# Strided heads of two batches regrouped by residue into small TensorE tiles, and local heads five chunks at a time

## The chip, the cores and the metric

One core of one Trainium2 chip runs the whole program in a single launch. The metric is the device time of that launch in microseconds. Three runs of the kernel before took 805.01, 805.74 and 808.72 us, a median of 805.74 us.

## What is computed

Attention with two kinds of heads, and then a token-and-channel mixer (an MLP over tokens, one over channels). Batch 8, 8 heads, 576 positions, 64 values per head:

```
scores = q @ k.T / 8
local heads 0-3:   key j counts for query i when 0 <= i-j < 32
strided heads 4-7: key j counts when j <= i and j % 32 == i % 32
attn = softmax(scores); x = attn @ v, heads side by side: x is [8, 576, 512]
h = relu(x.T @ w_tok1) @ w_tok2          (576 -> 256 -> 576 over tokens)
u = x + h.T
out = u + relu(u @ w_ch1) @ w_ch2        (512 -> 1536 -> 512 over channels)
```

## The kernel before, in words

The mixer works on fp32r pairs (a high and a low part, three matmuls for a product). It runs batch by batch: `mlp` (L705) takes 12 blocks of the hidden width, an up projection (`up_proj`, L720, 12 matmuls of 512 columns into the one PSUM bank `h`) and a down projection (`down_proj`, L742, 12 matmuls) each. A table `after` of this batch puts small pieces of other work between these steps: entry 3 is called when three projections have been written, and 3.5 in the middle of the fourth. The order on TensorE, VectorE, ScalarE and GpSimd is the order in which the code is written; before the first `mlp` that of the DMA queue on SyncE is too.

A strided head splits by residue: 32 residues, and 18 positions in each, so its scores are 32 causal blocks of 18x18. For batches 2 to 7 GpSimd and VectorE do them (`strided`, L388). For batches 0 and 1 TensorE does: `strided_pe` (L332) takes seven residues at once, so that 126x126 scores come out of one matmul, and the mask (an identity times `mask2_b`, L342, bf16) shuts what lies off the 18x18 diagonal blocks. One call handles one head (`j` of a pair `hp`) and the groups `gs`, three of them or two (`GS`, L616). It yields twice: after the scores and the exponential (L342 to L350), and after the transposes (L354) and their copy (L356); then come the products with the values (L360) and the division (L365 to L367). The result goes to the DRAM tensor `xd` (L372), and batch 0 loads it back into the SBUF tile `x` (`load_x`, L473).

Batch 0's local heads are done by `local_unit` (L180), for three or two chunks of 128 positions, in 64x32 tiles of the array: scores L197, transposes L224, values L232. Half a chunk belongs to batch 1; its first half is copied into `x` by DMA (L255). All this stands before the first `mlp`, together with the loading of the weights. A weight arrives as 64-bit floats and `convert` (L106) makes fp32r pairs of it, piece by piece: two operations on ScalarE (L128, L131), two on VectorE (L129, L133), then a cast on ScalarE (L142) and a subtraction on GpSimd (L143). The pieces are two and a short one of `t1` (w_tok1), two and a tail of `t2` (w_tok2), and of `w1` and `w2` (the channel weights); the first four of `w1` are also made here.

`tok1` (L481) splits the five chunks of `x` into high and low (L490, L496) and multiplies by `t1`; `hh` (L516) and `hl` (L517) are its result. `tok2` (L536) transposes one 128-column slice of `x` into PSUM, adds six matmuls with `t2` (L547), and `split_u` casts the sum to `uh` (L525, ScalarE) and `ul` (L526, VectorE), which the first `up_proj` reads.

Batch 1's strided heads are two `lanes` (L784), called in batch 0's `mlp` after steps 0 to 11 and half a step later, and what is left of batch 0's local heads (`rest`, L795) is called there as well. They share the three PSUM banks `t`.

Of the kernel before, what the change touches and what calls it, by code (L numbers as in the profile page):

```python
# [16 lines left out]
ALU = mybir.AluOpType  # L17
# [17 lines left out]
BUSY = 8  # L35
RG = 7
RP = RG * NJ
NRG = 5
NSB = 2
FIRST = {0: 1, 4: 2}  # L40
# [18 lines left out]
def attn_mixer_kernel(ctx, tc, qkT, vw, qkU, vU, qs, ks, vs, qksT, vsP, mask, mask2, w1, w2, wt1, wt2, outT):  # L59
# [14 lines left out]
    mask2_b = small[:RP, 64 + 16:64 + 16 + 3 * RP // 2].bitcast(BF16)  # L74
# [105 lines left out]
    def local_unit(pool, ps_t, p, hp, c0, n, into=None, single=(), masks=None, room=UC):  # L180

        one = dict.fromkeys(single, 1)
        qk_t = pool.tile([P, 2, room * P + 32], F32, name="lqk", bufs=one.get("lqk"))[:, :, :n * P + 32]
        q_t, k_t = qk_t[:, 0, 32:], qk_t[:, 1]
        v_t = pool.tile([P, 4 * room, DV], F32, name="lv")[:, :4 * n]
# [4 lines left out]
        if masks is not None:  # L190
            for j in range(2):
                nc.tensor.matmul(
                    sc[j][:, :64 * n], ident_b, masks[:, 64 * c0:64 * (c0 + n)], start=True, stop=False, skip_group_check=True)
        for t in range(4 * n):
            c, a = divmod(t, 4)
            for j in range(2):
                nc.tensor.matmul(  # L197
                    sc[j][32 * a:32 * a + 32, 64 * c:64 * c + 64],
                    q_t[64 * j:64 * j + 64, 32 * t:32 * t + 32], k_t[64 * j:64 * j + 64, 32 * t:32 * t + 64],
                    start=masks is None, stop=True, skip_group_check=True)  # L200
        s_t = pool.tile([P, room, 2, 64], F32, name="ls")
        m_t = pool.tile([P, room, 2], F32, name="lm")[:, :n]
        z_t = pool.tile([P, room, 2], F32, name="lz")[:, :n]
        if masks is not None:
            for j in range(2):
                s = sc[j][:, :64 * n].rearrange("p (c k) -> p c k", k=64)
                nc.vector.tensor_reduce(out=m_t[:, :, j], in_=s, axis=AX.X, op=ALU.max)
                nc.vector.tensor_tensor(
                    out=s_t[:, :n, j], in0=s, in1=m_t[:, :, j:j + 1].to_broadcast([P, n, 64]), op=ALU.subtract)
            s = s_t[:, :n].rearrange("p c j k -> p (c j k)")  # L210
            nc.scalar.activation(out=s, in_=s, func=AF.Exp, scale=SCALE)
        else:

            for c in range(n):
                for j in range(2):
                    nc.vector.tensor_tensor_reduce(
                        out=s_t[:, c, j, :], in0=sc[j][:, 64 * c:64 * c + 64], in1=mask_sb[:, FIRST.get(c0 + c, 0), :],
                        scale=-SCALE, scalar=TOP, op0=ALU.add, op1=ALU.min, accum_out=m_t[:, c, j:j + 1])
                    nc.scalar.activation(
                        out=s_t[:, c, j, :], in_=s_t[:, c, j, :], func=AF.Exp, bias=m_t[:, c, j:j + 1], scale=-1.0)  # L220
# [5 lines left out]
        nc.scalar.copy(out=pT[:, :n * P], in_=pt[:, :n * P])  # L226
# [12 lines left out]
        x_t = pool.tile([P, max(n - 1, 2) if into is not None or n < UC else UC, 2, D], F32, name="lx", bufs=one.get("lx"))  # L239
        cs = slice(P * hp, P * hp + P)  # L240

        nd = 0 if into is None else min(n, S // P - c0)
        for i0, i1 in ((0, nd), (nd, n)):
            for j in range(2):
                if i0 < i1:
                    to = x_t[:, i0:i1, j, :] if i0 >= nd else into[:, c0 + i0:c0 + i1, P * hp + D * j:P * hp + D * j + D]
                    nc.vector.tensor_tensor(
                        out=to, in0=av[j][:, i0:i1, :D],
                        in1=z_t[:, i0:i1, j:j + 1].to_broadcast([P, i1 - i0, D]), op=ALU.mult)
        if nd == n:  # L250
            return
        if nd:
            x = x_t[:, nd].rearrange("p j d -> p (j d)")
            for r in range(2):
                nc.sync.dma_start(out=into[64 * r:64 * r + 64, NSC - 1, cs], in_=x[:64])  # L255
            nc.sync.dma_start(out=xd[0][S:S + 64, cs], in_=x[64:])
            return
        nc.sync.dma_start(
            out=xd[p][P * c0:P * (c0 + n), cs].rearrange("(c p) d -> p c d", p=P), in_=x_t[:, :n].rearrange("p c j d -> p c (j d)"))
# [64 lines left out]
    def strided_load(pool, b, hp):  # L324
        one = 1 if b else 2
        qk_t = pool.tile([P, 2, S], F32, name="eqk", bufs=one)
        v_t = pool.tile([RP, NRG, 2, DV], F32, name="ev", bufs=one)
        nc.sync.dma_start(out=qk_t, in_=qksT[b, hp])
        nc.sync.dma_start(out=v_t, in_=vsP[b, hp])
        return qk_t[:, 0], qk_t[:, 1], v_t  # L330

    def strided_pe(pool, ps_t, b, hp, j, gs, loaded, outs):  # L332
        js = slice(64 * j, 64 * j + 64)
        q_t, k_t, v_t = loaded
        n = len(gs)

        rows = [min(RP, S - RP * g) for g in gs]
        sc = ps_t.tile([P, 512], F32, name="t")
        s_t = pool.tile([RP, 3, RP], F32, name="es", bufs=2 if b else 5)[:, :n]
        mz = pool.tile([RP, 2, 3], F32, name="em", bufs=2 if b else 5)[:, :, :n]  # L340
        m_t, z_t = mz[:, 0], mz[:, 1]
        nc.tensor.matmul(sc[:RP, :RP * n], ident_b[:RP, :RP], mask2_b[:, :RP * n], start=True, stop=False, skip_group_check=True)  # L342
        for i, g in enumerate(gs):
            r = rows[i]
            nc.tensor.matmul(  # L345
                sc[:r, RP * i:RP * i + r], q_t[js, RP * g:RP * g + r], k_t[js, RP * g:RP * g + r], start=False, stop=True, skip_group_check=True)
        s = sc[:RP, :RP * n].rearrange("p (c k) -> p c k", k=RP)
        nc.vector.tensor_reduce(out=m_t, in_=s, axis=AX.X, op=ALU.max)
        nc.vector.tensor_tensor(out=s_t, in0=s, in1=m_t.unsqueeze(2).to_broadcast([RP, n, RP]), op=ALU.subtract)
        nc.scalar.activation(out=s_t, in_=s_t, func=AF.Exp, scale=SCALE)  # L350
        yield
        pt = ps_t.tile([P, 512], F32, name="t")
        for i in range(n):
            nc.tensor.transpose(pt[:RP, RP * i:RP * i + RP], s_t[:, i], ident[:RP, :RP])  # L354
        pT = s_t
        nc.scalar.copy(out=pT, in_=pt[:RP, :RP * n].rearrange("p (c k) -> p c k", k=RP))  # L356
        yield
        av = ps_t.tile([P, 512], F32, name="t")
        for i, g in enumerate(gs):
            nc.tensor.matmul(av[:RP, DV * i:DV * i + DV], pT[:, i], v_t[:, g, j], start=True, stop=True)  # L360
        if j == 0:
            outs[gs] = pool.tile([RP, n, 2, D], F32, name=f"ex{n}", bufs=1 if b else 2)
        x_t = outs[gs]
        a = av[:RP, :DV * n].rearrange("p (c d) -> p c d", d=DV)
        nc.vector.tensor_scalar_add(z_t, a[:, :, D], 1e-9)  # L365
        nc.vector.reciprocal(out=z_t, in_=z_t)
        nc.vector.tensor_tensor(out=x_t[:, :, j], in0=a[:, :, :D], in1=z_t.unsqueeze(2).to_broadcast([RP, n, D]), op=ALU.mult)  # L367
        if j == 1:

            to = x_strided(b, P * hp, P).rearrange("(j r) d -> r j d", r=ST)  # L370
            for i, g in enumerate(gs):
                nc.sync.dma_start(out=to[RG * g:RG * g + rows[i] // NJ], in_=x_t[:rows[i], i].rearrange("p j d -> p (j d)"))  # L372
        yield


# [240 lines left out]
    GS = ((0, 1, 2), (3, 4))  # L616
    with tc.tile_pool(name="first", bufs=4) as first, \
         tc.tile_pool(name="raws", bufs=4, side="right") as raws, \
         tc.tile_pool(name="ps_a", bufs=6, space=PSUM) as ps_a, \
# [3 lines left out]
        mask2_sb = first.tile([RP, RP], F32, name="mask2_sb", bufs=1)  # L623
        masks = first.tile([P, 5 * 64], BF16, name="masks", bufs=1)
        nc.sync.dma_start(out=mask2_sb, in_=mask2)
        loaded = [strided_load(first, 0, hp) for hp in range(2)]
        nc.sync.dma_start(out=mask_sb, in_=mask)
        nc.gpsimd.tensor_copy(
            out=mask2_b.rearrange("p (c k) -> p c k", k=RP), in_=mask2_sb.unsqueeze(1).to_broadcast([RP, 3, RP]))
        for c in range(5):  # L630
            nc.gpsimd.tensor_copy(out=masks[:, 64 * c:64 * c + 64], in_=mask_sb[:, FIRST.get(c, 0)])
# [7 lines left out]

        keep_busy(WARM)  # L640
# [5 lines left out]
        for hp in range(2):  # L646
            outs = {}
            work += [strided_pe(first, ps_a, 0, hp, j, gs, loaded[hp], outs) for j in range(2) for gs in GS]
# [17 lines left out]
        for i in range(len(work) + 4):  # L666
            for k in (0, 2, 4):
                if 0 <= i - k < len(work):
                    if k == 2 and i >= BUSY:
                        keep_busy(2)  # L670
# [329 lines left out]
```

## Time and profile before

| | |
|---|---|
| median of three runs | 805.74 us |
| the profiled execution | 805.1 us, its span 803.3 us |
| TensorE busy | 781.1 us (97%) |
| VectorE, ScalarE, GpSimd busy | 476.6, 247.9, 378.0 us |
| first matmul of the first up projection | 52.92 us |
| granted TensorE clock | 1.00 in every stretch |
| DMA | 96.17 MB, mean 120 GB/s |

Busy time counts a matmul from its issue to its modelled end, and matmuls overlap, so "busy" alone does not say that the array is full. The chain that ended last gives TensorE 76% of the span, VectorE 10%, GpSimd 5%, DMA 4%.

### The profile page before, as it was taken

The page shows a single profiled execution, that of the slowest core. Times are in us where ns is not written, and L with a number is a line of the kernel's source. Part 1 is how long each engine was busy: PE and PEld are TensorE (multiplying, and loading weights), DVE is VectorE, ACT ScalarE, POOL GpSimd, SP SyncE. Part 2 cuts the span into 40 slices and gives each one's busy share as a digit, 9 for nine tenths or more (in the row PEclk, how much of TensorE's full clock was granted, in tenths as well). Part 3 has the DMA queues.
Part 4 walks back from the last instruction along what each step waited for, and adds up shares of the span by engine and source line. Part 5 has one row for each costly group of instructions (what it writes and reads, how often), then busy time and mean ns, then how long its engine had stood idle before and what let it go on. Part 6 is the DMA issues. An engine that isn't in the chain of part 4 may idle for free.

```text
span 803.3 us, 14310 instructions
## 1 busy us (share of the span) xinstructions
PE 781.1 (97%) x5714; PEld 632.0 (79%) x5718; DVE 476.6 (59%) x1030; ACT 247.9 (31%) x515; POOL 378.0 (47%) x285
## 2 busy tenths in 40 slices
PE   9789999999999999999999999999999999999998
PEld 6567776877778888888788888788888888888886
DVE  6856766778598677776687657776652233113112
ACT  5668765232122322331223122332222212102010
POOL 2223345959776883778558856766600000202000
PEclk9999999999999999999999999999999999999999
DMA  9676545234812282247215520655042212101001
GB/s 312 194 255 208 188 147 193 92 130 138 261 40 95 85 238 67 109 113 262 94 53 173 148 82 12 215 163 158 1 125 75 83 47 73 53 0 53 1 0 53
DMA packets 70782, 96.17 MB, mean 120 GB/s; under 512 B 33604, under 2 KB 42948, under 8 KB 70716
## 3 DMA queue, kind: packets, MB, share of 16 engines
q1 hardware_dynamic: 70140, 93.36, 37.3%
q10 hardware_dynamic: 576, 1.90, 0.6%
q8 instruction: 45, 0.74, 0.4%
q14 instruction: 21, 0.17, 0.1%
HBM read 67.65 MB, written 27.46 MB: 118 GB/s over the span
## 4 chain that ended last, share of the span: by engine, by line
PE 76%; DVE 10%; POOL 5%; DMA 4%; issue 2%; ACT 2%; SPq 1%; DVEq 0%; ACTq 0%; POOLq 0%
PE acc L740 30%; PE h L728 27%; PE t L547 5%; POOL sprod L383 4%; PE t L508 4%; PE t L728 3%; DMA w_raw<-in_w 2%; PE t L345 1%; DVE sa L463 1%; PE t L303 1%; DMA x<-x 1%; DVE xhl L496 1%; DVE w_f L133 1%; PE t L279 1%; DVE gl L732 1%
## 5 line engine op out<-in xcount | busy, mean ns | idle before, releaser
L383 POOL TENSOR_TENSOR sprod<-sa,ss 128x576 f32<-128x576 f32 (+8 forms) x108 | 153.3, 1457 | 84.8 <-issue 48.8
L383 POOL TENSOR_TENSOR sprod<-sa 128x576 f32<-128x576 f32 (+8 forms) x108 | 160.5, 1519 | 37.4 <-DVE ss L436 11.6
L740 PE MATMUL acc<-gh,w2h 128*128 128x512 f32 x432 | 170.7, 395 | 0.0
L732 DVE SCALAR_TENSOR_TENSOR gl<-h,gh 128x512 fp32r<-128x512 f32 x99 | 68.0, 687 | 172.9 <-ACT gh L731 172.8
L740 PE MATMUL acc<-gl,w2h 128*128 128x512 f32 x432 | 168.4, 390 | 0.0
L740 PE MATMUL acc<-gh,w2l 128*128 128x512 f32 x432 | 168.4, 390 | 0.0
L728 PE MATMUL h<-uh,w1h 128*128 128x512 f32 x396 | 157.9, 399 | 2.5 <-DVE gl L732 2.5
L728 PE MATMUL h<-ul,w1h 128*128 128x512 f32 x396 | 154.5, 390 | 0.0
L728 PE MATMUL h<-uh,w1l 128*128 128x512 f32 x396 | 154.5, 390 | 0.0
L731 ACT ACTIVATE gh<-h 128x512 fp32r<-128x512 f32 x99 | 59.0, 596 | 290.0 <-PE h L728 289.8
L436 DVE TENSOR_REDUCE ss<-sprod 128x9 f32<-128x576 f32 (+8 forms) x108 | 80.4, 777 | 28.0 <-POOL sprod L383 27.9
L740 PEld LDWEIGHTS acc<-gh,w2l 128*128 128x128 f32 x432 | 81.1, 188 | 17.2
L740 PEld LDWEIGHTS acc<-gh,w2h 128*128 128x128 f32 x432 | 81.1, 188 | 17.1
L740 PEld LDWEIGHTS acc<-gl,w2h 128*128 128x128 f32 x432 | 81.1, 188 | 16.4 <-DVE gl L732 0.3
L728 PEld LDWEIGHTS h<-uh,w1h 128*128 128x128 f32 x396 | 74.3, 188 | 20.5 <-DVE gl L732 4.1
L463 DVE TENSOR_REDUCE sa<-sprod 128x64 f32<-128x576 f32 (+8 forms) x108 | 80.1, 776 | 17.2 <-POOL sprod L383 16.8
L728 PEld LDWEIGHTS h<-ul,w1h 128*128 128x128 f32 x396 | 74.3, 188 | 16.0
L728 PEld LDWEIGHTS h<-uh,w1l 128*128 128x128 f32 x396 | 74.4, 188 | 14.5
L575 POOL TENSOR_TENSOR x<-x,xhl 128x512 f32<-128x512 f32 x4 | 5.0, 1288 | 115.2 <-DMA x<-u 115.2
L508 PE MATMUL t<-xhl,t1h 128*128 128x512 f32 x134 | 42.3, 398 | 4.7 <-DVE xhl L493 2.5
L496 DVE TENSOR_TENSOR xhl<-x,xhl 128x512 fp32r<-128x512 f32 x30 | 31.1, 1055 | 10.7 <-ACT xhl L490 10.7
L490 ACT CAST xhl<-x 128x512 fp32r<-128x512 f32 x37 | 22.3, 620 | 43.3 <-PE t L508 36.9
(141 smaller groups left out, 915.2 us busy)
## 6 DMA issues: line engine op xcount, KB each, us to landing
out_t<-ot SPq DMA_DIRECT2D x35, 256.0 KB
w_raw<-in_w SPq DMA_DIRECT2D x17, 512.0 KB
lqk<-in_qkU SPq DMA_DIRECT2D x9, 832.0 KB
x<-x SPq DMA_DIRECT2D x28, 256.0 KB
lv<-in_vU SPq DMA_DIRECT2D x9, 780.0 KB
xhl<-in_w SPq DMA_DIRECT2D x7, 512.0 KB
x<-lv SPq DMA_DIRECT2D x36, 96.0 KB
xtl<-lv SPq DMA_DIRECT2D x36, 96.0 KB
```

Source lines behind the costliest of these rows:

```text
L133: nc.vector.scalar_tensor_tensor(out=a, in0=a, scalar=3, in1=y, op0=ALU.logical_shift_left, op1=ALU.bitwise_xor)
L383: i = nc.gpsimd.tensor_tensor(op=op, **operands)
L436: nc.vector.tensor_reduce(out=s_t[:, i, :i + 1], in_=pr.rearrange("p (n d) -> p n d", d=D), axis=AX.X, op=ALU.add)
L463: nc.vector.tensor_reduce(out=o_t[:, i], in_=pr.rearrange("p (d n) -> p d n", n=i + 1), axis=AX.X, op=ALU.add)
L490: nc.scalar.copy(out=xh, in_=x)
L496: apart.append(nc.vector.tensor_tensor(out=xlo, in0=x, in1=xh.bitcast(F32), op=ALU.subtract))
L508: nc.tensor.matmul(ph[m], l[:, c, P * m:P * m + P], r, start=(c == 0 and k == 0), stop=(c == NSC - 1 and k == 1))
L547: nc.tensor.matmul(pu, l[:, cs], r[:, m, :MAIN], start=(turned and m == 0 and k == 0), stop=(m == 1 and k == 2), skip_group_check=True)
L728: nc.tensor.matmul(ph, l[:, cc, fs], r, start=(cc == 0 and k == 0), stop=(cc == NCC - 1 and k == 2))
L731: nc.scalar.activation(out=gh, in_=ph, func=AF.Relu)
L732: nc.vector.scalar_tensor_tensor(out=gl, in0=ph, scalar=0.0, in1=gh.bitcast(F32), op0=ALU.max, op1=ALU.subtract)
L740: nc.tensor.matmul(acc[cc], l[:, fc, cs], r, start=(fc == 0 and k == 0), stop=(fc == NFC - 1 and k == 2))
```

## The change

The strided heads of batches 0 and 1 are laid out in another way. The 32 residues are split into four groups of eight (`NB`); group `a` writes to PSUM partitions 32a to 32a+31, of which 18 are used. One matmul makes the scores of one residue of one head: 64 rows, 32 weight columns (18 used), 18 moving columns, in a 64x32 tile, 64 matmuls for a pair of heads. Four 128x128 transposes follow for the pair, and 64 matmuls with the values with 18 rows each, in two halves (`l0`). The values come with 18 partitions per load in four loads per pair, and the result leaves in four stores per pair. Both heads of a pair go through one reduction, one subtraction and one exponential.

```diff
-    def strided_pe(pool, ps_t, b, hp, j, gs, loaded, outs):
...
+    def strided_pe(pool, pair, one, b, hp, loaded, s_t):
+        qk_t, v_t, _ = loaded
+        sc, both = pair()
+        for j in range(2):
+            nc.tensor.matmul(sc[j][:, :NB * NJ], ident_b, mask2_b, start=True, stop=False, skip_group_check=True)
+        for n in range(NB):
+            h, l = divmod(n, 4)
+            for a in range(4):
+                r = NB * a + 2 * l + h
+                for j in range(2):
+                    js = slice(64 * j, 64 * j + 64)
+                    nc.tensor.matmul(
+                        sc[j][32 * a:32 * a + 32, NJ * n:NJ * n + NJ],
+                        qk_t[js, NJ * r:NJ * r + 32], qk_t[js, S + NJ * r:S + NJ * r + NJ], start=False, stop=True, skip_group_check=True)
...
+        for g in range(4):
+            nc.tensor.transpose(pt[:, P * g:P * g + P], s_t[:, P * g:P * g + P], ident)
+        nc.scalar.copy(out=s_t, in_=pt)
+        yield
+        x_t = pool.tile([P, NB, 2 * D], F32, name="ex")
+        for l0 in (0, 2):
+            av, both = pair()
+            for g in range(4):
+                j, h = divmod(g, 2)
+                for a in range(4):
+                    for l in range(2):
+                        ls = slice(32 * (l0 + l), 32 * (l0 + l) + NJ)
+                        at = DV * (2 * h + j)
+                        nc.tensor.matmul(
+                            av[l][32 * a:32 * a + 32, at:at + DV], s_t[ls, P * g + 32 * a:P * g + 32 * a + 32], v_t[ls, 2 * h + j, a],
+                            start=True, stop=True, skip_group_check=True)
...
+            if l0:
+                to = x_strided(b, P * hp, P).rearrange("(j r) d -> j r d", r=ST)
+                for a in range(4):
+                    nc.sync.dma_start(out=to[:, NB * a:NB * a + NB], in_=x_t[32 * a:32 * a + NJ])
+            yield
```

Batch 0's local heads become `local_first`: one call for a pair of heads takes all five chunks at once, its scores, transposes and values in two PSUM banks each, which are one tile called `pair`. `local_unit` keeps only the later chunks, as `local_rest`. Before the first `mlp` PSUM is now three such pairs (`ps_p`, bufs=3); the token mixer's four accumulators are halves of pairs (`Halves`). The order of the start is written anew, and batch 1 has one lane in place of two:

```diff
+        class Halves:
+            left = []
+            def tile(self, shape, dtype, name):
+                if not self.left:
+                    t = ps_p.tile([P, 2, 512], F32, name="pair")
+                    self.left += [t[:, 0], t[:, 1]]
+                return self.left.pop(0)
...
+        steps(l0)
+        loaded[1][2]()
+        steps(l1, l0, l1, *early[:4])
+        keep_busy(2)
+        steps(s0, s1)
+        keep_busy(2)
+        steps(s0, l0, s1, s0, s0, l1, s1, s1)
+        load_x(x_t, 0, slice(HL * D, DM))
+        steps(l0, early[0], l1, early[1], early[0], l0, early[4])
+        keep_busy(2)
+        steps(early[1], early[2], l1, early[5], early[2], early[6])
...
-        mixes = [tok2(up0, ps_a, x_t, h, cc, u, False) for cc in range(NCC)]
+        mixes = [tok2(up0, halves, x_t, h, cc, u, False) for cc in range(NCC)]
         steps(mix)
-        keep_busy(8)
-        steps(*mixes, early[8], mix, early[6], mix, mix, early[6], early[7], mix, mix, early[7], *pieces[:4])
-        steps(mixes[0], mixes[1], early[8], mixes[2], pieces[0], mixes[3], early[8])
+        keep_busy(4)
+        steps(early[7], mixes[0], mixes[1], mix, early[3], early[3], mix, early[4], mixes[2], mixes[3], early[4], early[8], mix, early[5], mix, mix, early[5], early[6], *pieces[:4])
+        steps(mixes[0], mixes[1], early[6], early[7], mixes[2], early[7], early[8], mixes[3], pieces[0], early[8])
...
-            for k, g in enumerate(lanes):
-                for i in range(12):
-                    at(i + 0.5 * k, next, g, None)
+            for i in (0, 1, 2, 3, 4, 4.5, 7, 8, 9, 10):
+                at(i, next, lanes[0], None)
```

TensorE in batch 0's first projections, before: `strided_pe` of batch 1 comes per head and group, L342 being the mask, L345 the scores, L354 the transposes, L360 the values; the "..." are matmuls of the projections.

```order
L342 LDWEIGHTS small
L342 MATMUL t<-small 126x378
L345 MATMUL t<-eqk 126x126 x3
...
L342 LDWEIGHTS small
L342 MATMUL t<-small 126x252
L345 MATMUL t<-eqk 126x126
L345 MATMUL t<-eqk 72x72
...
L354 MATMUL t<-ident,es 126x126 x3
...
L360 MATMUL t<-ev,es 126x65 x3
```

The same place in the change, where L364 is the mask, L371 the scores, L388 the transposes and L400 the values:

```order
L364 LDWEIGHTS small
L364 MATMUL t<-small 128x144
L364 LDWEIGHTS small
L364 MATMUL t<-small 128x144
L371 MATMUL t<-eqk 32x18 x64
...
L388 MATMUL t<-ident,es 128x128 x4
...
L400 MATMUL t<-ev,es 32x65 x32
...
L400 MATMUL t<-ev,es 32x65 x32
```

Eight sequences (four heads, two groups of residues each) became two, one for each pair of heads, of many small matmuls.

ScalarE around the split of `x` (L490) before. The two pieces of `t2` are cast ahead of it, and one piece of `w1`:

```order
L142 CAST t2h<-w_f 128x512
L142 CAST w1h<-w_f 128x2x256
L490 CAST xhl<-x 128x512 x2
L490 CAST eqk<-x 128x512 x2
L490 CAST lv<-x 128x512
L128 ACTIVATE w_rest_101<-w_raw,small 128x512
L131 ACTIVATE w_f<-w_raw 128x512
L142 CAST w1h<-w_f 128x2x256
L128 ACTIVATE w_rest_102<-w_raw,small 128x512
L131 ACTIVATE w_f<-w_raw 128x512
L516 ACTIVATE hh_155<-t 128x512
L516 ACTIVATE hh_157<-t 128x512
```

In the change (L533 is the split, L125, L128 and L139 make a piece of a weight, L559 is `hh`):

```order
L533 CAST lv<-x 128x512
L125 ACTIVATE w_rest_102<-w_raw,small 128x512
L128 ACTIVATE w_f<-w_raw 128x512
L139 CAST t2h<-w_f 128x512
L125 ACTIVATE w_rest_101<-w_raw,small 128x512
L128 ACTIVATE w_f<-w_raw 128x512
L139 CAST t2h<-w_f 128x512
L125 ACTIVATE w_rest_102<-w_raw,small 128x512
L128 ACTIVATE w_f<-w_raw 128x512
L559 ACTIVATE hh_161<-t 128x512
L559 ACTIVATE hh_163<-t 128x512
L139 CAST w1h<-w_f 128x2x256
```

Both pieces of `t2` and all four of `w1` now stand behind the last cast of `x`.

TensorE in `tok2` of the change, with the waits of each row; a slice of `u` takes six such rows, and these are the first slice's last two, the second slice's first two, and the first of the third slice and of the fourth (L547 before has no wait behind its first six rows):

```order
L590 MATMUL pair<-t2l,hh_163 128x512 [waits Pool_49]
L590 MATMUL pair<-t2h,hl_164 128x512 [waits DVE_49]
L590 MATMUL pair<-t2h,hh_161 128x512 [waits DVE_49]
L590 MATMUL pair<-t2l,hh_161 128x512
...
L590 MATMUL pair<-t2h,hh_161 128x512
...
L590 MATMUL pair<-t2h,hh_161 128x512 [waits DVE_49]
```

The second and the fourth slice, which are the second halves of their pairs, got a wait for VectorE.

## Rows read from the trace of the kernel before

**Rows 1.** The page, busy time by engine.

```profile
PE 781.1 (97%) x5714; PEld 632.0 (79%) x5718; DVE 476.6 (59%) x1030; ACT 247.9 (31%) x515; POOL 378.0 (47%) x285
```

**Rows 2.** Busy time by stretch: us, length, engines' busy us (instructions), clock, DMA share, GB/s.

```profile
55.50:112.00 56.50, 54.72 (x523) 43.28 (x522) 39.22 (x128) 42.44 (x88) 19.57 (x16) 1.00 0.58 183
```

**Rows 3.** The chain that ended last, 39 to 56 us: start, us, what.

```profile
39.79 1.88 DMA x<-lx
...
41.82 0.62 ACT lv L490
42.44 0.78 ACT w_rest L128
43.22 0.52 ACT w_f L131
...
43.76 0.70 DVE w_f L133
...
44.49 0.62 ACT w1h L142
...
46.39 0.48 ACT hh L516
...
46.92 6.00 PE t L547 x24
52.92 2.72 PE h L728 x12
```

**Rows 4.** The same chain, 55.4 to 69.6 us.

```profile
55.64 0.16 PE t L342
55.80 0.85 PE t L345 x6
56.65 1.60 PE t L728 x6
58.25 0.11 PE t L342
58.37 0.54 PE t L345 x4
...
60.49 0.33 PE t L354 x3
...
65.45 0.61 PE t L360 x6
66.06 1.45 PE acc L740 x6
67.50 0.39 PE t L360 x4
```

**Rows 5.** The same chain at 76.65 us, a local unit's scores.

```profile
76.65 0.38 PE t L197 x32
```

**Rows 6.** Timeline of TensorE: start, us, what, idle before it.

```profile
1.19 3.95 PE L638 MATMUL t<-still 128*128 128x512 bf16 x10 [1.19 <-DVE still L622]
...
46.92 0.50 PE L547 MATMUL t<-t2h,hh 128*128 128x512 f32 x1 [2.51 <-ACT hh L516]
...
101.10 0.27 PE L197 MATMUL t<-lqk 64*32 64x64 f32 x2 [1.32 <-issue]
```

**Rows 7.** Timeline of VectorE in the first 56 us.

```profile
6.27 0.55 DVE L348 TENSOR_REDUCE em<-t 126x3 f32<-126x378 f32 x1 [5.14 <-PE t L345]
...
24.39 0.35 DVE L207 TENSOR_REDUCE lm<-t 128x3 f32<-128x192 f32 x1
...
28.12 0.29 DVE L367 TENSOR_TENSOR ex<-t,em 126x128 f32<-126x128 f32 x1
...
49.96 0.69 DVE L526 TENSOR_TENSOR ul<-t,uh 128x512 fp32r<-128x512 f32 x1 [1.18 <-ACT uh L525]
```

**Rows 8.** Timeline of the DMA queue on SyncE: issues.

```profile
28.84 1.45 SPq L372 DMA_DIRECT2D x<-ex x2
...
33.56 1.77 SPq L476 DMA_DIRECT2D x<-x x4
```

More of the change, by code (lines that the diff above doesn't have):

```diff
@@ L189, in local_unit @@
         sc = [ps_t.tile([P, 512], F32, name="t") for _ in range(2)]
[L190 to L193, printed above, removed]
         for t in range(4 * n):
@@ L199, in local_unit @@
                     q_t[64 * j:64 * j + 64, 32 * t:32 * t + 32], k_t[64 * j:64 * j + 64, 32 * t:32 * t + 64],
[L200 to L204, printed above, removed]
-            for j in range(2):
[L206 to L220, printed above, removed]
+                    start=True, stop=True, skip_group_check=True)
+        s_t = pool.tile([P, n, 2, 64], F32, name="ls")
+        m_t = pool.tile([P, n, 2], F32, name="lm")
+        z_t = pool.tile([P, n, 2], F32, name="lz")
+        for c in range(n):
+            for j in range(2):
+                nc.vector.tensor_tensor_reduce(
+                    out=s_t[:, c, j, :], in0=sc[j][:, 64 * c:64 * c + 64], in1=mask_sb[:, FIRST.get(c0 + c, 0), :],
+                    scale=-SCALE, scalar=TOP, op0=ALU.add, op1=ALU.min, accum_out=m_t[:, c, j:j + 1])
+                nc.scalar.activation(
+                    out=s_t[:, c, j, :], in_=s_t[:, c, j, :], func=AF.Exp, bias=m_t[:, c, j:j + 1], scale=-1.0)
         yield
@@ L238, in local_unit @@
         nc.vector.reciprocal(out=z_t, in_=z_t)
[L239 to L257, printed above, removed]
+        x_t = pool.tile([P, n, 2, D], F32, name="lx", bufs=1)
+        for j in range(2):
+            nc.vector.tensor_tensor(
+                out=x_t[:, :, j, :], in0=av[j][:, :, :D], in1=z_t[:, :, j:j + 1].to_broadcast([P, n, D]), op=ALU.mult)
         nc.sync.dma_start(
-            out=xd[p][P * c0:P * (c0 + n), cs].rearrange("(c p) d -> p c d", p=P), in_=x_t[:, :n].rearrange("p c j d -> p c (j d)"))
+            out=xd[p][P * c0:P * (c0 + n), P * hp:P * hp + P].rearrange("(c p) d -> p c d", p=P), in_=x_t.rearrange("p c j d -> p c (j d)"))
     def local_wide(pool, ps_t, p, unit):
@@ L324, in strided_load @@
     def strided_load(pool, b, hp):
-        one = 1 if b else 2
-        qk_t = pool.tile([P, 2, S], F32, name="eqk", bufs=one)
-        v_t = pool.tile([RP, NRG, 2, DV], F32, name="ev", bufs=one)
+        qk_t = pool.tile([P, 2, S], F32, name="eqk")
+        v_t = pool.tile([P, 4, 4, DV], F32, name="ev")
         nc.sync.dma_start(out=qk_t, in_=qksT[b, hp])
-        nc.sync.dma_start(out=v_t, in_=vsP[b, hp])
-        return qk_t[:, 0], qk_t[:, 1], v_t
-    def strided_pe(pool, ps_t, b, hp, j, gs, loaded, outs):
[L333 to L350, printed above, removed]
-        yield
[L352 to L356, printed above, removed]
-        yield
[L358 to L373, printed above, removed]
@@ L614, in do_pieces @@
                 next(pieces[k])
[L616 to L617 removed]
+    with tc.tile_pool(name="first", bufs=2) as first, \
          tc.tile_pool(name="raws", bufs=4, side="right") as raws, \
[L619 removed]
+         tc.tile_pool(name="ps_p", bufs=3, space=PSUM) as ps_p, \
          tc.tile_pool(name="ps_m", bufs=2, space=PSUM) as ps_m:
@@ L638, in keep_busy, with pair, one @@
                 nc.tensor.matmul(idle_t, still[:, :P], still, start=True, stop=True)
+        class Halves:
[5 more added lines that the diff above has]
+                return self.left.pop(0)
+        def pair():
+            t = ps_p.tile([P, 2, 512], F32, name="pair")
+            return (t[:, 0], t[:, 1]), t
+        def one():
+            return ps_p.tile([P, 2, 512], F32, name="pair")[:, 0]
         keep_busy(WARM)
@@ L643, in attn_mixer_kernel @@
         h = new_h(xp)
-        units = [local_unit(first, ps_a, 0, hp, c0, n, x_t, masks=masks) for c0, n in ((3, 2), (0, 3)) for hp in range(2)]
-        work = []
-        for hp in range(2):
-            outs = {}
-            work += [strided_pe(first, ps_a, 0, hp, j, gs, loaded[hp], outs) for j in range(2) for gs in GS]
-        work += units
+        s0, s1 = (strided_pe(first, pair, one, 0, hp, loaded[hp], e_ts[hp]) for hp in range(2))
+        l0, l1 = (local_first(first, ps_p, 0, hp, x_t, masks) for hp in range(2))
         early = [t1_piece(raws, 0), t1_piece(raws, 2), t1_short(raws), t2_piece(raws, 0), t2_piece(raws, 1)]
```

163 lines of the change are left out of this document (121 added, 42 removed).

## The prediction

> **What bounds the kernel now.** I read the page first: TensorE is busy for 97% of the span, every other engine far less [rows 1]. The share alone says little, so next comes the chain of waits, to see which engine ends each stretch. From the first up projection at 52.92 us on [rows 3] it is nearly all TensorE: twelve matmuls of 512 columns in 2.72 us, 0.227 us each, and between them the pieces of batch 1's attention [rows 4]. In 55.5 to 112 us, where these pieces stand, TensorE has 54.7 of 56.5 us busy [rows 2], and its timeline shows one real hole, 1.32 us at 101.10 [rows 6]. Whatever leaves TensorE there shortens the run by as much. Before 52.92 us it is different: there VectorE, DMA and ScalarE end the waits in turn. The last part of that chain is the reader's key to the start [rows 3]: a DMA brings the last rows of `x` (39.79 to 41.67), ScalarE casts them at 41.82, makes the first half of a weight piece, another cast, `hh` at 46.39, and TensorE's 24 `tok2` matmuls take 6.00 us. The first up projection ends at 52.92 + 2.72 = 55.64, that is 13.8 us behind the cast at 41.82; I call the time of that cast T. So the change has two accounts: TensorE's work behind 55.64, and the date of that point.
>
> **First account: batch 1 on TensorE.** What goes, for one head [rows 4]: mask and scores of three groups 0.16 + 0.85, of two groups 0.11 + 0.54; the six projection matmuls behind them take 1.60 where half of 2.72 is 1.36, so 0.24 more each time; transposes 0.33 for three and so 0.22 for two; values 0.61 + 0.39, with 1.45 - 1.36 = 0.1 lost behind them. Sum 1.25 + 0.89 + 0.55 + 1.1 = 3.8 us, four heads 15.2 us.
>
> What comes, for a pair of heads: two masks, 0.3 (0.11 to 0.16 each [rows 4]). 64 score matmuls: the nearest row is the local unit's, also in 64x32 tiles, 32 records in 0.38 us [rows 5]; a matmul in fp32 leaves two records, so 24 ns a matmul, and 64 take 1.54, plus 0.24 behind them. Four transposes at 0.33/3 [rows 4], 0.44. Values: two runs of 32 matmuls, at the same 24 ns 0.77 each, plus 0.24 behind each. Sum 0.3 + 1.78 + 0.44 + 2.02 = 4.5 us, two pairs 9.1 us. **Saved: 6.1 us.**
>
> Two prices are not in the trace. A score matmul has 18 moving columns where the row has 64: at worst it costs the same 24 ns, at best in proportion 7 ns, which would save 2.2 us more over 128 of them. I take 24, the price of the only row with tiles of this form. [...] The value matmuls have 18 weight rows in a 32-row group where the row has 64: at best 24 ns, at worst one after the other as with the big ones, 0.61/3 = 0.20 us [rows 4]. I take 24, since these again lie in different tiles and banks; the other end is a rival.
>
> The hole at 101 us comes from a wait for a `t` bank that VectorE still reads. The change takes two banks at once for scores and values, and I expect about as much waiting at steps 1.5 and 7.5, where a local unit wants two banks 1.4 us behind a pair's scores; I put the difference at nothing, plus or minus 1.5. VectorE, ScalarE and SyncE's queue lose or gain a few us in this stretch under TensorE (39 and 42 of 56.5 us busy [rows 2]): no cost.
>
> **Second account: the start.** When is T? The strided results of batch 0 leave at 28.4 us now [rows 7], since 40 short VectorE operations and the local units stand ahead of them. In the change a pair takes one reduction and one subtraction of 288 elements and two times three operations. By the rows, about 1 ns an element (0.55 for 378, 0.35 for 192 [rows 7]) on 0.15: 0.45 each; 0.82 for a local pair's 640; about 1.0 for a half's sum, reciprocal and product. TensorE has the first scores near 7 us. VectorE is then through with both pairs' scores at 9.7, with the first local pair's at 13.1 (its loads are larger and land near 10), with the first strided result at 15.1, the second local pair's scores at 17.7, and the second strided result at 19.7. That is 8.7 us earlier. Four stores of about 0.9 us (now 1.45 for two, one of them short [rows 8]) end at 23.4. From the end of the last store's issue, 30.3, to the first reload at 33.56 it takes 3.2 us now [rows 8], so the reload begins near 26.6. From there to T it takes 41.82 - 33.56 = 8.3 us for six reloads and the local tail's copies; a weight load of 0.45 stands among them in the change. **T = 35.3, 6.5 us earlier.**
>
> What is late next is ScalarE, and this eats the gain. Both `t2` pieces and all four `w1` pieces stand behind the cast at T. A piece, one after the other, is 2.67 us from its first operation to the end of its cast (42.44 to 45.11 [rows 3]). Counted from T: the cast 0.6; two `t2` pieces 5.3, to 5.9; the first two operations of a `w1` piece 1.3, to 7.2; then `hh`, and TensorE starts `tok2` at 7.8 (5.1 now). Two `hl` on VectorE bring 9.1, that piece's VectorE operation and cast 10.3, the next piece's two operations 11.6, `uh` (0.6, as the cast at T) and `ul` (0.69 [rows 7]) 12.9. Here the new wait strikes: the second slice is the other half of the same tile, so its six matmuls (1.4) begin only now and end at 14.4; `uh`, `ul` 15.8; the piece's VectorE operation and cast 17.0; two operations 18.3; `uh`, `ul` of the third slice 19.5; the fourth slice's matmuls run beside a VectorE operation, a cast and two operations, to 22.1; its `uh`, `ul` 23.4. The up projection's last three matmuls need that. It ends at **T + 23.6 = 58.9 us, 3.3 us later than now.**
>
> **Sum.** 805.1 - 6.1 + 3.3 = 802.3 us against the profiled execution; the median of the runs lies 0.6 above that, so I forecast 802.5 us. Behind 112 us I move nothing: what waits there on weights and on GpSimd begins with the projections and shifts with them. About 0.5% (4.0 us) is what a measurement can tell from no change.
>
> **Rivals.**
> *Both accounts gain* (0.36): if the start's chain is no longer than now, because T comes near 32 or the pieces of `w1` overlap better than one by one, the point at 55.64 stays or moves up by 1 us, and short columns may add 2 us: 796 to 799.5 us. For it speaks that ScalarE has holes while it waits for `x`; against it, that its order puts the pieces behind.
> *Small tiles don't overlap* (0.08), slower: 128 value matmuls of batch 1 at 0.20 us in place of 0.024 are 22.5 us in the dense stretch, 825 us. It decides from 77 ns a matmul on: 128 x 53 ns = 6.8 us more than my forecast is 0.5% over now. For it: no row shows 18 weight rows. Against it: 24 ns with 64 rows [rows 5].
> *Late start* (0.09): if the reload is not earlier (T = 41.8), the sum is 808.8 us. TensorE's clock can do a part of it: its first ten matmuls of 512 columns are 0.38 us apart [rows 6], not 0.227, although the profile shows a granted clock of 1.00. In the change TensorE stands idle from the end of `tok1` (cast, its VectorE operation and four matmuls behind T, 2.3) to T + 7.8, 5.5 us against 2.51 now [rows 6]; 24 matmuls at 0.38 cost 3.7 us. [...]
>
> **How the numbers follow.** My forecast has 0.47, with a range of its own from 800 to 805.5: T plus or minus 1.5, the bank waits plus or minus 1.5. A tenth of it (0.04) lies below the bound for faster. Faster: 0.36 + 0.04 = 0.40. Slower: the tiles 0.08 and half of the late start 0.05, 0.13. Same: 0.43 + 0.04 = 0.47. The range of 8 in 10 takes in the first rival and the late start: 795.5 to 809.5.
>
> **What the profile of the change should show.** 128 records of scores per pair in about 1.5 us and 64 per value run in 0.8 (much longer: the tile rival). The cast of the last `x` rows near 35 us. `tok2` begun near 43, with holes of over 1 us on TensorE ahead of its second slice and in the first up projection; that projection ended near 59. Batch 1's attention over in some 48 us of TensorE's time from there. I am wrong if the first up projection ends before 55 or after 62 us, or if the stretch behind it is not 4 to 8 us shorter.

## The result, and the profile after the change

The changed kernel takes **818.91 us** (median of 4 runs, 816.37 to 820.68) against 806.12 us for the kernel before (805.01 to 808.72): a ratio of **1.0145, 95% interval 1.0119 to 1.0171**, 12.8 us slower. I had forecast 802.5, with a range from 795.5 to 809.5. The profiled execution took 820.68 us; its span is 818.9 us.

The page of the changed kernel answers to [rows 1]. TensorE has 2.5 us less work, in 819 matmul records more. The line of the granted clock (40 slices of some 20 us) begins with 8677 where it was 9 throughout.

```profile
PE 778.6 (95%) x6533; PEld 627.1 (77%) x6536; DVE 462.7 (56%) x968; ACT 239.2 (29%) x487; POOL 378.7 (46%) x286
...
PEclk8677999999999999999999999999999999999999
...
q8 instruction: 51, 0.84, 0.4%
```

The chain of waits from T, the cast of `x`'s last rows, to the first up projection answers to [rows 3] (start, us, what). T is at 46.85 us, not at 41.82, and the projection ends at 70.62 + 4.13 = 74.75 us, not at 55.64.

```profile
46.85 0.61 ACT lv L533
...
59.64 2.94 PE pair L590 x6
...
67.69 2.93 PE pair L590 x6
70.62 4.13 PE h L784 x12
```

So the start lost 19.1 us. From there to batch 1's first `tok1` matmul it is 65.3 us (140.01 - 74.75) where it was 67.3 (122.95 - 55.64): the dense stretch gave back 2.0. Together 17.1; the two profiled spans differ by 15.6.

The reason for the late T stands in TensorE's timeline of the first 30 us (start, us, what, number of records, idle time before it and who ended it).

```profile
5.94 1.27 PE L371 MATMUL pair<-eqk 64*32 64x18 f32 x128
...
7.37 0.85 PE L371 MATMUL pair<-eqk 64*32 64x18 f32 x79
12.04 0.71 PE L371 MATMUL pair<-eqk 64*32 64x18 f32 x49 [3.82 <-issue]
13.09 0.63 PE L684 MATMUL t<-still 128*128 128x512 bf16 x1 [0.33 <-issue]
13.51 1.06 PE L388 MATMUL pair<-ident,es 128*128 128x128 f32 x4
14.37 0.74 PE L188 MATMUL pair<-masks,small 128*128 128x320 bf16 x2
15.04 1.08 PE L192 MATMUL pair<-lqk 64*32 64x64 f32 x71
18.79 0.44 PE L192 MATMUL pair<-lqk 64*32 64x64 f32 x9 [2.67 <-issue]
19.16 1.11 PE L388 MATMUL pair<-ident,es 128*128 128x128 f32 x4
20.20 1.92 PE L400 MATMUL pair<-ev,es 18*32 18x65 f32 x114
26.40 0.46 PE L400 MATMUL pair<-ev,es 18*32 18x65 f32 x14 [4.28 <-issue]
26.79 0.71 PE L188 MATMUL pair<-masks,small 128*128 128x320 bf16 x2
27.44 1.41 PE L192 MATMUL pair<-lqk 64*32 64x64 f32 x80
28.77 0.68 PE L400 MATMUL pair<-ev,es 18*32 18x65 f32 x31
29.67 1.63 PE L400 MATMUL pair<-ev,es 18*32 18x65 f32 x97 [0.22 <-issue]
```

Three gaps of 3.82, 2.67 and 4.28 us lie inside runs of like matmuls, where the operands of the next record are those of the last or were written together with them, and all say "issue": TensorE waited for nothing that the profile shows. Count the records from gap to gap: 49+1+4+2+71 = 127, 9+4+114 = 127, 14+2+80+31 = 127; the weight loads in the same three stretches are 128, 126 and 128 (now and then the trace lacks a record). The page's third part has a queue for instructions, 51 packets in 0.84 MB, so 16 KB each; 6533 matmul records over 51 packets are 128 for each. In slices of 0.1 us one of its packets shows up at 16.3, one at 23.9 (the row below) and one at 9.5 us, each time 2.4 to 2.5 us ahead of the end of a gap.

```profile
q8 instruction: 1, 0.02, 64.4%
```

**The theory** that I tested next: TensorE's program comes in pieces of 128 matmul records, each with its weight load. A piece is fetched while the one before it runs (the only packet between 26.40 and 29.67 us shows up at 27.4, behind the start of the piece of 26.40 and ahead of the next). A piece of 128 small records runs through in 1.2 us (5.94 to 7.14 above), and then TensorE stands still until the next has come. No run here shows more than one piece fetched ahead.

What the wait depends on shows in the stretches (us, length, busy us, last three columns: granted clock, DMA share, GB/s). From the start of one piece until the next is there it takes 18.79 - 12.04 = 6.75 us and 26.40 - 18.79 = 7.61 us while the loads fill the DMA engines (share 1.02; the second wait runs on to 26.4 us although the share is 0.33 from 22), but 29.67 - 26.40 = 3.27 us behind them. And behind each of the three gaps the granted clock is 0.50 (in 12.04 to 15.04, 18.79 to 22 and 26.4 to 35 us), even where TensorE has 8.35 of 8.6 us busy.

```profile
5.00:22.00 17.00, 10.17 (x469) 7.91 (x468) 3.98 (x9) 2.46 (x5) 0.95 (x5) 0.81 1.02 297
22.00:26.40 4.40, 0.12 (x7) 0.00 (x1) 0.56 (x1) 0.23 (x1) 0.00 (x0) 0.50 0.33 104
26.40:35.00 8.60, 8.35 (x314) 6.60 (x316) 5.68 (x14) 3.08 (x5) 0.00 (x0) 0.50 0.27 60
```

In batch 1's stretch there is one more such gap in the middle of four transposes, again with a granted clock of 0.50 behind it (111 to 114 us; 0.42 us from `acc` matmul to `acc` matmul instead of 0.23):

```profile
107.42 0.38 PE L388 MATMUL t<-ident,es 128*128 128x128 f32 x2
110.12 0.44 PE L388 MATMUL t<-ident,es 128*128 128x128 f32 x2 [2.32 <-issue]
...
111.19 0.63 PE L796 MATMUL acc<-gh,w2h 128*128 128x512 f32 x1
111.61 0.63 PE L796 MATMUL acc<-gl,w2h 128*128 128x512 f32 x1
```

### The profile page after: what moved, and what is told of

The parts are those of the page before. It is cut to its first block, busy times and chain, and to the rows that moved or that the text cites. A ratio compares the mean times of both kernels' runs of the same rounds, so it can differ in the third digit from the quotient of the medians.

```text
span 818.9 us, 15839 instructions
## 1 busy us (share of the span) xinstructions
PE 778.6 (95%) x6533; PEld 627.1 (77%) x6536; DVE 462.7 (56%) x968; ACT 239.2 (29%) x487; POOL 378.7 (46%) x286
## 4 chain that ended last, share of the span: by engine, by line
PE 73%; DVE 9%; POOL 4%; ACT 3%; DMA 3%; issue 2%; SPq 1%; DVEq 0%; ACTq 0%; POOLq 0%
PE acc L796 30%; PE h L784 27%; PE t L590 4%; POOL sprod L426 4%; PE t L551 4%; PE t L784 2%; DMA x<-x 1%; DVE xhl L539 1%; DVE sa L506 1%; PE t L327 1%; DVE ss L479 1%; DVE gl L788 1%; PE t L303 1%; DMA x<-lx 1%; DVE w_f L130 1%
## 5 line engine op out<-in xcount | busy, mean ns | idle before, releaser
L533 ACT CAST xhl<-x 128x512 fp32r<-128x512 f32 x37 | 22.3, 620 | 43.6 <-PE t L551 36.0
```

The costliest lines, as they stand in the source:

```text
L533: nc.scalar.copy(out=xh, in_=x)
```

## Experiments

The ratios are against the kernel before, run on the same chip; its medians there were 807 to 809 us.

**Each half of the change alone.** Batch 1's heads with the old start, then the new start with batch 1's old blocks. The edits swap the functions `strided_load` and `strided_pe`, their layout of the values and their mask, for one of the two batches; the lane's steps follow:

```diff
-lanes = [strided_lane(second, 1, gs, got) for gs in GS]
+lanes = [strided_lane(One(second), 1)]
```

> Only batch 1's strided heads are changed; the start is the old one. Theory A (PE's instructions come in pieces of 128 matmul records, and a piece that is used up faster than the next one arrives leaves PE idle; nearly all of that is at the start): the first up projection ends where it did before (55 to 56.5 us), the stretch behind it is 3 to 6 us shorter, 800 to 803 us, with at most one or two idle gaps of about 2 us inside runs of small matmuls. Rival B (the small matmuls themselves cost more than the wide ones they replace, wherever they stand): the stretch behind the first up projection is no shorter, 806 to 812 us.

Measured: 803.77 us, **0.9967 (0.9942 to 0.9993)**, just above the 800 to 803 that I had expected. The first up projection ends at 56.48 us. Behind it TensorE has two gaps with an instruction packet 2.4 us ahead of their end (1.59 us to 64.44 and 0.53 to 93.34) and one of 1.63 for a bank.

> Only the start is changed; batch 1's strided heads keep their old blocks. Theory A: the same idle gaps as in the change at the start (about 11 us in all), the first up projection ends near 74.6 us, and the run is 815 to 825 us. Rival B: the loss is shared between the start and batch 1, so the start alone gives at most half of it, 808 to 814 us.

Measured: 826.62 us, **1.0236 (1.0214 to 1.0259)**, gaps of 3.95, 2.64 and 3.86 us, the projection's end at 75.76 us. The loss is the start's, and even more than I had expected; the rival with dear matmuls falls, since batch 1's small matmuls alone made the run shorter. The two ratios don't add up to the change's 1.0145: with the new start behind it, the new lane was worth 7 us, alone 2.7.

**Where the gaps sit.** 32 more matmuls behind the warm-up:

```diff
 keep_busy(WARM)
+for _ in range(32):
+    nc.tensor.matmul(idle_t[:, :32], still[:, :P], still[:, :32], start=True, stop=True)
```

> The change with 32 more small bf16 matmuls on zeros right behind the warm-up. Theory A: the idle gaps move by 32 matmul records in the program: the first comes behind 47 records of the second pair of heads' scores (79 in the change), the second behind 39 of the five chunks' scores (71), the third behind 82 of the products with the values (114). Rival C (a gap belongs to its operation or to its moment: a bank, a data wait that the profile does not show, the DMA load at that time): the gaps stay behind 79, 71 and 114 records, or at the same times.

TensorE's timeline of this kernel, the three gaps:

```profile
8.36 0.58 PE L371 MATMUL pair<-eqk 64*32 64x18 f32 x47
12.26 0.97 PE L371 MATMUL pair<-eqk 64*32 64x18 f32 x81 [3.31 <-issue]
...
15.50 0.77 PE L192 MATMUL pair<-lqk 64*32 64x64 f32 x39
19.00 0.78 PE L192 MATMUL pair<-lqk 64*32 64x64 f32 x41 [2.73 <-issue]
...
20.76 1.47 PE L400 MATMUL pair<-ev,es 18*32 18x65 f32 x82
26.51 0.96 PE L400 MATMUL pair<-ev,es 18*32 18x65 f32 x46 [4.27 <-issue]
```

47, 39 and 82 records, to the record: each gap has moved by exactly 32 places in the program. It belongs to the count of instructions, not to an operation, a bank or a load. The gaps end within 0.3 us of the old times (12.26, 19.00, 26.51 us), as they would if the arrival of a packet ends them; a gap that belonged to its moment alone would not have kept 128 records to the next. One count holds all through: in each of the nine kernels with the new start or the matmuls added below, the first of these gaps stands behind 223 matmul records (12+2+128+2+79 in the timeline above). (One run, 822.59 us.)

**Why a piece is late.** Four weight loads of the start, 1.7 MB, issued behind the first strided stores:

```diff
-steps(l1, l0, l1, *early[:4])
+steps(l1, l0, l1)
...
-steps(s0, l0, s1, s0, s0, l1, s1, s1)
+steps(s0, l0, s1, s0, s0, *early[:4], l1, s1, s1)
```

> The change with the first four early weight loads (1.7 MB) issued behind the stores of the first strided results instead of before any work. Theory A with the DMA queues as the reason why a piece arrives late: the third gap (4.3 us at 22.1 us, while the loads still fill the queues) shrinks to under 2 us, the first (3.8 us) stays and the second (2.7 us) changes by less than 1 us; T, the cast of x's last rows (46.8 us), comes 1 to 4 us earlier, unless the weights are then late; 815 to 819 us. Rival D (a piece takes as long whatever the queues do): the gaps stay within 0.5 us of 3.8, 2.7 and 4.3 us.

```profile
18.82 0.44 PE L192 MATMUL pair<-lqk 64*32 64x64 f32 x9 [2.43 <-issue]
...
22.86 0.46 PE L400 MATMUL pair<-ev,es 18*32 18x65 f32 x14 [0.71 <-issue]
```

The first two gaps stay (3.85, 2.43), the third shrinks from 4.28 to 0.71: that piece came 4.04 us after the one before had begun instead of 7.61, with a DMA share of 0.58 in 15 to 20 us and 0.07 in 20 to 26. So with few loads left on the DMA engines this piece came 3.57 us sooner. This is one execution, and the length of a gap varies between executions: in the run with wide matmuls on zeros below, whose start is the change's, the three were 5.18, 1.59 and 2.29 us. But no other kernel with the new start has a third gap under 2 us. The run gained nothing, 819.87 us, 1.0159 (1.0141 to 1.0176): the strided results left VectorE 3.5 us earlier, but their second stores and then the reloads of `x` now stood behind the weights in the queues, and T stayed at 46.74 us. That was a bad place for the loads.

**The gap put into the kernel before.** 128 small matmuls on zeros in its start:

```diff
 for i in range(len(work) + 4):
+    if i == 4:
+        tiny(128)
```

> The kernel before with 128 small fp32 matmuls on zeros (256 records, 64x32 tiles of 18 columns) added to its start, about 11 us into the run, while the loads fill the DMA queues. Theory A (PE's instructions arrive in pieces of 128 records, 3.3 us after the piece before has begun when the queues are free and 6.5 to 7.6 us when they are full): two more idle gaps of 3 to 5 us inside the added run of matmuls, the issue gaps of the start sum to 8 to 13 us (3.2 before), and the run is 4 to 9 us longer, 810 to 815 us. Rival B (what the matmuls cost is their own time): 2.4 to 4 us of PE, no new gap, at most 3 us longer.

```profile
9.66 1.73 PE L645 MATMUL t<-still 64*32 64x18 f32 x184
16.45 1.16 PE L645 MATMUL t<-still 64*32 64x18 f32 x72 [5.05 <-issue]
```

The stretches of the same kernel behind it:

```profile
9.00:17.00 8.00, 2.95 (x231) 2.61 (x234) 1.25 (x3) 1.52 (x4) 0.95 (x5) 0.88 1.06 363
17.00:36.00 19.00, 18.67 (x185) 15.61 (x179) 10.94 (x35) 7.69 (x16) 2.84 (x3) 0.51 0.51 156
```

One gap, not two: by the theory the piece that begins 56 records into the run, where TensorE has no gap, had been fetched ahead, and only the one after it (128 later, 5.05 us) had not; and 39 records before the run and 184 in it are the 223 again. But the run took 820.94 us, **1.0175 (1.0156 to 1.0194)**, twice what I had expected: behind the gap the granted clock is 0.51 for 19 us although TensorE is busy for 18.67 of them, and T comes at 55.35 us, 13.5 later. 2.9 us of matmuls that compute nothing, put in this place, cost as much as the whole change did (its interval overlaps the change's). How much of it is the low clock and how much the gap no run separates.

**What stands behind T.** The `t2` weight pieces converted in ScalarE's idle time ahead of the splits of `x`, and no two neighbouring slices in one tile:

```diff
-if not self.left:
-    t = ps_p.tile([P, 2, 512], F32, name="pair")
-    self.left += [t[:, 0], t[:, 1]]
-return self.left.pop(0)
+if len(self.left) < 3:
+    self.left.append(ps_p.tile([P, 2, 512], F32, name="pair"))
+    return self.left[-1][:, 0]
+return self.left[0][:, 1]
...
-steps(s0, l0, s1, s0, s0, l1, s1, s1)
+steps(s0, l0, s1, s0, s0, early[0], early[3], early[0], early[3], early[4], l1, s1, s1)
...
```

> The change with the two token-mixing weight pieces of the second step converted in ScalarE's idle time ahead of the splits of x, and with the four slices of the second step placed so that no slice waits for the split of the slice before it. Theory A: the gaps of PE at the start stay (10 to 12 us), T stays at 46 to 49 us, and from T to the end of the first up projection it takes 14 to 17 us instead of 27.7: it ends at 61 to 65 us, and the run is 807 to 812 us. Rival E (the wait behind T comes from something else: the low clock, the DMA loads of the weights): T to the end of the first up projection stays above 22 us, 815 to 820 us.

Measured: 811.2 us, 1.0049 (1.0031 to 1.0067). The gaps stay (3.81, 2.82, 4.68). T is at 46.72, the projection's last matmul begins at 66.21 us, T + 19.5: shorter by 8 us, though not by as much as I said, because VectorE's `ul` still follows ScalarE's `w1` pieces (2.67 us of waiting ahead of the projection). The clock is at 1.00 from 50 us on in this kernel, so this gain holds a part of the next one.

**The clock.** 42 wide matmuls on zeros in TensorE's idle time behind `tok1`:

```diff
...
+idle_t = one()
+keep_busy(22)
+steps(mixes[0])
+keep_busy(8)
-steps(mixes[0], mixes[1], early[6], early[7], mixes[2], early[7], early[8], mixes[3], pieces[0], early[8])
+steps(mixes[1], early[6], early[7], mixes[2], early[7], early[8])
+keep_busy(12)
+steps(mixes[3], pieces[0], early[8])
```

> The change with 42 wide matmuls on zeros in PE's idle time behind the first token-mixing step (22 ahead of the first slice, 8 ahead of the second, 12 ahead of the fourth). Theory A with the clock as a term of its own: the granted clock stays at 0.9 or more between 50 and 75 us, matmuls are 0.23 us apart instead of 0.43, the first up projection ends 3 to 5 us earlier (69.5 to 71.5 us), and the run is 814 to 817 us. Rival F (the low clock hides behind waits of ScalarE and VectorE): no earlier than 73.5 us, 818 to 820 us.

```profile
48.55 4.92 PE L684 MATMUL pair<-still 128*128 128x512 bf16 x21
53.92 0.50 PE L590 MATMUL pair<-t2h,hh 128*128 128x512 f32 x1 [0.45 <-ACT hh L559]
54.25 0.40 PE L590 MATMUL pair<-t2l,hh 128*128 128x512 f32 x1
```

Measured: 815.05 us, 1.0101 (1.0080 to 1.0122), with a clock of 1.00 from 50 to 75 us; the projection's last matmul ends at 69.76 + 0.39 = 70.15 us, 4.6 earlier, of which 0.7 is an earlier T. More matmuls, less time. In the gaps of the start no run tried wide matmuls of this kind; by theory A TensorE has no instructions to run there.

**The local part of the start.** Batch 0's local heads in three and two chunks again, the rest of the change kept:

> The change without its part on batch 0's local heads: they go in units of three and two chunks again, at the same places of the start; the strided heads of both batches stay changed. Theory A (the small matmuls of the strided heads use up the pieces; the local heads have as many records either way): the three gaps of 3.8, 2.7 and 4.3 us stay within 0.8 us each, T is at 46 to 49 us, 817 to 823 us. Rival H (the five chunks over two banks cost much of the loss): the gaps sum to under 8 us or T comes before 44.5 us, under 815 us.

Measured: 818.72 us, 1.0134 (1.0106 to 1.0163), T at 46.42 us, as expected of theory A; but the gaps are 4.78 and 4.22 us (behind 223 and 478 records, as in the change), and the middle one is gone (between its two neighbours the matmuls came in shorter runs, with a wait of 0.47 us for a load, and 5 us went by before the next piece was wanted). The five chunks over two banks cost or bring nothing that can be measured.

**Can batch 1's part be had without gaps?** The change of batch 1 alone leaves TensorE idle for 3.9 of the 50 us from 60 to 110. A first spreading of the local chunks' steps:

> Only batch 1's strided heads are changed, as in the run that changed them alone, and batch 0's last local chunks are moved by up to one and a half blocks so that their small matmuls don't follow the strided heads' within half a block. Theory A: the gaps of that run between 55 and 110 us (1.6, 0.5 and 1.6 us for a bank) go or fall under 0.5 us each, and the run is 2 to 4 us shorter than it: 0.992 to 0.995 of the kernel before. Rival G (the gaps are hidden by other waits, or come back at the new places): no shorter than that run, 0.996 to 0.998.

Measured: 805.96 us, 0.9991 (0.9974 to 1.0009). The issue gaps were gone from that stretch, but waits for ScalarE of 1.36 and 1.57 us had come in their place, where two steps of one unit now lay half a block apart. So the second spreading kept a whole block between most steps of either (the edit is against the change of batch 1 alone):

```diff
-for i in (0, 1, 2, 3, 4, 4.5, 7, 8, 9, 10):
+for i in (0, 1, 2, 3, 4, 4.5, 7.5, 8.5, 9.5, 10.5):
...
-((0, 1.5, 2.5, 3.5), (2, 4.5, 5.5, 6.5), (5, 7.5, 8.5, 9.5), (7, 9.5, 10.5, 11.5))
+((0, 2.5, 3.5, 4.5), (3, 5, 6, 7), (5.5, 8, 9, 10), (8.5, 9, 10, 11))
```

> Only batch 1's strided heads are changed, with the steps of both lanes a whole block apart, so that neither a run of small matmuls nor a wait for ScalarE or for a bank follows within half a block. Theory A: no issue gap over 0.5 us between 55 and 110 us, and none of the waits of 1.4 to 1.6 us that took their place in the first spreading; PE's idle time between 60 and 110 us falls from 3.9 us to under 2 us: 0.991 to 0.995 of the kernel before. Rival G (a lane's small matmuls always wait for something near there): idle time of 3.5 us or more, 0.996 to 1.000.

Measured: **802.21 us, 0.9930 (0.9907 to 0.9953)**: faster than both kernels. Busy time by stretch, first the batch 1 change alone, then this spreading:

```profile
60.00:110.00 50.00, 46.09 (x862) 34.60 (x851) 32.10 (x112) 35.15 (x71) 18.59 (x15) 1.00 0.63 200
```

```profile
60.00:110.00 50.00, 49.30 (x931) 36.90 (x907) 33.51 (x116) 36.69 (x74) 19.34 (x17) 1.00 0.69 218
```

TensorE's idle time fell from 3.91 to 0.70 us.

**The whole change with both repairs** (order and second spreading):

> The whole change with both repairs that do not touch the gaps of the start: the order of ScalarE's weight pieces and of the slices, and both lanes' steps a whole block apart. What it still loses against the kernel with batch 1's heads alone and the same spacing (0.993 of the kernel before) is what the start's three gaps cost. Theory A: the three gaps stay (10 to 12 us), the first up projection ends at 65 to 67.5 us, 9 to 11 us later than in that kernel, and the run is 0.998 to 1.003 of the kernel before: 5 to 8 us behind that kernel. Rival I (with the order mended and the clock up, little is lost): under 0.996.

Measured: 813.38 us, 1.0061 (1.0042 to 1.0081), outside what I expected. The gaps are there (3.88, 2.66, 4.34), the projection's last matmul begins at 65.53 us, some 9 us later than in the kernel of the second spreading, as said. The remaining miss is new: this start and this spreading together make TensorE wait for a weight piece of GpSimd,

```profile
103.94 0.50 PE L796 MATMUL acc<-gh,w2l 128*128 128x512 f32 x1 [3.35 <-POOL w2l L140]
```

which neither repair alone shows. GpSimd's piece was written at 103.88 us, but an instruction packet also began at 101.48 us, 2.46 us ahead of the end of this gap and it stands behind 1616 weight loads, as the gap of 2.32 us does in the changed kernel. So the wait for the piece and a wait for instructions ended together, and the profile names one of them; which repair would remove it is open. A version in which the changed start is no loss I did not find; that the gaps' length follows the loads was shown for the third one only.

## Why the prediction was wrong, by its steps

**The prices of the small matmuls held.** These rows are from batch 1's stretch in the changed kernel:

```profile
87.38 0.86 PE L400 MATMUL t<-ev,es 18*32 18x65 f32 x64
88.16 0.50 PE L784 MATMUL h<-uh,w1h 128*128 128x512 f32 x1
...
102.74 1.27 PE L371 MATMUL t<-eqk 64*32 64x18 f32 x128
103.94 0.50 PE L784 MATMUL h<-uh,w1h 128*128 128x512 f32 x1
```

64 score matmuls of 18 columns take 1.20 us (128 records, 102.74 to 103.94), 19 ns each where I took 24; 32 value matmuls 0.78 us (87.38 to 88.16), 24 ns as assumed. The score records are 9.4 ns apart, the value records 12. My rival "small tiles don't overlap", with 200 ns for a value matmul, is excluded by the same rows.

**The step that failed is "VectorE is then through with both pairs' scores at 9.7 ... and the second strided result at 19.7".** It took for granted that TensorE delivers a run of small matmuls at 24 ns each as soon as the data is there. It holds no term for the supply of instructions. The last strided product ended at 31.94 + 0.69 = 32.6 us:

```profile
31.94 0.69 DVE L412 TENSOR_TENSOR ex<-pair,em 128x512 f32<-128x512 f32 x1
```

Of the 12.9 us, 10.8 are the three gaps; the other 2.1 were not taken apart (the lower clock behind the gaps is my guess). T follows almost one to one: 46.85 against the 35.3 predicted, and 41.82 before. The signs were there: the old start has two such gaps, of 1.42 us inside 48 like matmuls (21.92 to 23.33) and of 1.44 (to 33.91), with an instruction packet 2.4 to 2.6 us ahead of the end of each; I took them for noise.

```profile
23.33 0.33 PE L197 MATMUL t<-lqk 64*32 64x64 f32 x11 [1.42 <-issue]
...
33.91 1.67 PE L638 MATMUL t<-still 128*128 128x512 bf16 x7 [1.44 <-issue]
```

The hole at 101.10 us in [rows 6], also marked "issue", has no such packet near it.

**The walk behind T held, the clock in it did not.** `tok2` was to begin at T + 7.8, and it began at 54.60, T + 7.75; the second slice at T + 12.9, and it came at 59.64, T + 12.8. From there most of TensorE's matmuls ran 0.43 us apart instead of 0.23 (six in 2.94 us, twelve in 4.13, against 2.72 for twelve in [rows 3]), and the end came at T + 27.9, not T + 23.6. (By its own terms the walk ends at T + 24.1, since the last three matmuls behind 23.4 take 0.68 us and not 0.2.) The difference is the term that I had put into the rival "late start", at 3.7 us, rather than into the sum. The run with wide matmuls on zeros shows it: with the clock at 1.00 from 50 to 75 us, its projection ends at 70.15 us, with T at 46.11, so at T + 24.0. That an idle time of this length lowers the clock no trace had shown me: behind the 2.51 us ahead of `tok2` it was 1.00 before, and the 0.38 us that I took for the slow matmuls stood beside a granted clock of 1.00 too [rows 6]. In the changed kernel the granted clock is 0.50 in 54.6 to 60 us, behind TensorE's idle time of 5.17 us ahead of `tok2`, and still 0.65 in 70.42 to 74.75, the up projection. Behind the gaps of the start, marked "issue", it is 0.50 as well.

```profile
54.60 0.79 PE L590 MATMUL pair<-t2h,hh 128*128 128x512 f32 x1 [5.17 <-ACT hh L559]
```

**The first account was right in size, not in what reaches the end.** I had set the waits beside it at "nothing, plus or minus 1.5". In the changed kernel they were the gap of 2.32 us, 0.97 for a bank, and about 1.6 of half clock behind the gap (eight matmuls 0.2 us slower each), 4.9 us where the hole of 1.32 [rows 6] and 0.45 behind it had been; of the 6.1 us 2.0 were left. TensorE's whole account of the stretch, before and after (columns as above, TensorE's busy us first):

```profile
55.64:122.95 67.31, 65.29 (x569) 51.82 (x568) 44.74 (x137) 49.77 (x98) 25.89 (x21) 1.00 0.62 195
```

```profile
74.75:140.01 65.26, 61.35 (x984) 46.17 (x984) 38.60 (x125) 45.19 (x86) 25.25 (x21) 0.97 0.67 213
```

Its busy time fell by 3.9 us, so by 5.5 without the half clock, where I had 6.1, and its idle time rose from 2.0 to 3.9. With the steps a block apart the saving reaches the end, 0.9930 or 5.7 us, though a part of that is the old hole, which this spreading closes too.

**The sum.** Predicted 805.1 - 6.1 + 3.3, and 0.6 for the median, which makes 802.9 and not the 802.5 that I wrote down. Measured in the profiled execution: 805.1 - 2.0 + 19.1, less 1.5 that comes back behind batch 1's first `tok1` matmul, 820.7. The 19.1 are the 3.3 predicted, 11.5 for the later T and 4.3 for the clock behind it. Both of the prediction's signs of being wrong came: the projection ended after 62 us, and the stretch behind it was 2.0 us shorter, not 4 to 8.

## What to carry to other kernels

Price a run of small matmuls twice: by what the array takes, and by what it takes to bring the instructions; here 128 records took 3.3 us to come with a DMA share of 0.13, and at the start, between two gaps, 5.5 us (the run with wide matmuls on zeros) to 7.9 (the run with the other order). With wide matmuls between the small ones, a block apart in the second spreading, TensorE was idle for only 0.70 of 50 us. So cut work into small tiles where wide matmuls stand between the pieces rather than at a start that lives on DMA; even there the gap of 2.32 us in batch 1's stretch says that the spacing has to be tried out. And a gap marked "issue" inside a run of like instructions is worth counting records for before anything else.

## What I had not expected of the hardware

In the kernel before, one gap for want of instructions cost about twice its length: 5.05 us of it at 11 us left the granted clock at 0.51 from 17 to 36 us with TensorE busy throughout, and the run 13.3 us longer, of which 2.9 are the added matmuls themselves. And small fp32 matmuls in neighbouring tiles start 9.4 ns apart per record, faster than the nearest row of the kernel before (32 records in 0.38 us, 12 ns [rows 5]) had let me assume.
